# Linear attention into a soft mixture of experts: early loads joined, two batches' key-value products a tile later, one weight unit loaded by itself

## The chip, the core and the metric

The kernel runs on one core of one Trainium2 chip. The metric is device microseconds of one execution; the median of three runs stands for the kernel.

## What is computed

```python
def _attn_ref(q, k, v, g_norm):                       # q, k, v: 8 batches x 8 heads x 576 x 64
    kv = np.einsum('bhsd,bhse->bhde', k, v)
    out = np.einsum('bhsd,bhde->bhse', q, kv)
    rms = np.sqrt(np.mean(out * out, axis=-1, keepdims=True) + 1e-06)
    return (out / rms * g_norm).astype(np.float32)

def _moe_ref(x, phi, w1, w2):                         # x: 4608 x 512, 8 experts, 4 slots each, 1024 wide
    logits = x @ phi
    d = np.exp(logits - logits.max(0, keepdims=True))
    d /= d.sum(0, keepdims=True) + 1e-09
    slot_input = (d.T @ x).reshape(E, S_per_e, D)
    for e in range(E):
        h = np.maximum(slot_input[e] @ w1[e], 0.0)
        slot_out[e] = h @ w2[e]
    c = np.exp(logits - logits.max(1, keepdims=True))
    c /= c.sum(1, keepdims=True) + 1e-09
    return (c @ slot_out.reshape(n_slots, D)).astype(np.float32)
```

The attention's output, its heads side by side, is x. All is float32.

## The kernel before

x is worked on in 36 tiles of 128 tokens (`NT`). Nine tiles are two batches; tile 4 of each nine holds the ends of both. For a tile, `products` multiplies the queries with `bds[b % 2]`, a block matrix that holds a batch's key-value product and that product times phi; the result goes to one of two pairs of PSUM banks. ScalarE then squares it (`square`) and copies it out (`evict`), VectorE reduces the squares and the partial logits, GpSimd scales. Softmax over the tokens runs along in groups of six tiles (`group_max` to `group_sum`).

A batch's key-value product is made by `kv_step` in three steps: step 0 is 16 products of its first half, step 1 is 16 of its second half with 8 for the borders and a copy by ScalarE, step 2 (`slots`) transposes and fills `bds`. The table `kv_steps` (lines 625 to 628) says ahead of which tile a step stands: the key is the batch and the tile counted from the batch's first tile, `first`, which is 4 for batch 1 and 9 for batch 2. So before, step 0 of batch 1 stands ahead of tile 2 and steps 1 and 2 ahead of tile 3; the three steps of batch 2 stand ahead of tiles 6, 7 and 8. Batch 0 is done half by half ahead of tile 0 (lines 677 to 684).

After the last tile come the experts: `expert_h(e)` multiplies with w1, `expert_y(e, half)` with w2, then `gather`, `mix` and `output` write the result through four stores.

All data goes through `arena`, 160 units of 256 columns, whose parts serve one thing after the other (`KV_AT`, `Q_AT`, `W_AT`). All transfers are issued by SP, in the order in which the code stands. `load_row` loads keys, values and queries; eight such loads are issued at the start without a wait, three more behind batch 0, one behind tile 9. `load_w` loads a row of `W_ROWS`, several weight units that lie side by side, and is called behind tiles 18, 24 and 27 (`loads_behind`) and from the last part. The row that begins with half of w2's unit 2 takes units 32 to 72 of the arena, and so waits for the last reads of the last queries, which lie at 36 to 54.

The class `Order` records every operation with the cells it reads and writes, and `emit` gives each operation the waits that follow from this. A load has one semaphore; whoever reads any part of it waits for all of it. All operations are issued from one helper, so all rows of the profile say line 204.

Of the kernel before, what the change touches and what calls it, by code (L numbers as in the profile page):

```python
# [11 lines left out]
P = 128  # L12
# [15 lines left out]
TOK = 4608  # L28
# [4 lines left out]
KV_AT = (0, 36, 54, 0, 90, 126, 18, 54)  # L33
Q_AT = (18, 72, 108, 36)
# [6 lines left out]
    (("w1", 0, None), ("w1", 1, None)),  # L41
    (("w1", 2, None), ("w1", 3, None)),
    (("w1", 4, None), ("w2", 2, 1), ("w2", 0, None), ("w2", 1, None)),
    (("w2", 2, 0), ("w1", 6, None), ("w1", 5, None)),
    (("w1", 7, None),),
    (("w2", 3, None), ("w2", 4, None)),
    (("w2", 5, None), ("w2", 6, None)),
# [5 lines left out]
HEAD = 144  # L53
# [207 lines left out]
def row_length(row):  # L261
    return sum(UNIT if part is None else UNIT // 2 for _, _, part in row)


def soft_moe_linear_attention(nc, first_in, kv_in, q0_in, q1_in, kv4_in, kv5_in, t3_in, w_in, out):


    const = Const(nc)
# [9 lines left out]
    def place(at, n):  # L278
        return arena[:, HEAD + at * KB : HEAD + at * KB + n]

    def load_row(at, src):
        nc.sync.dma_start(place(at, src.shape[-1]), src)
# [14 lines left out]
    def homes(kind, u):  # L297
        at = W_AT[kind, u]
        if at is None:
            return [xflat[:, :UNIT]]  # L300
        return [place(a, UNIT // len(at)) for a in at]

    def load_w(kind, u, part=None):
        i = [row[0] for row in W_ROWS].index((kind, u, part))
        lo = sum(row_length(row) for row in W_ROWS[:i])
        n = row_length(W_ROWS[i])
        src = w_in[:, lo * P : (lo + n) * P].rearrange("o (p n) -> (o p) n", p=P)
        t = homes(kind, u)[part or 0]
        if n > t.shape[-1]:
            t = place(W_AT[kind, u][part or 0], n)  # L310
        nc.sync.dma_start(t, src)

    def w_block(kind, u, i):
# [4 lines left out]


    nc.sync.dma_start(arena[:, : HEAD + 2304], first_in)  # L320
    load_row(KV_AT[0] + 9, kv_in[0, :, 2304:])
    load_row(Q_AT[0], q0_in[:, :2048])
    load_row(KV_AT[1], kv_in[1, :, :2304])
    load_row(KV_AT[1] + 9, kv_in[1, :, 2304:])
    load_row(Q_AT[0] + 8, q0_in[:, 2048:])
    load_row(KV_AT[2], kv_in[2])
    load_row(Q_AT[1], q1_in)


    loads_behind = {  # L330
# [1 line left out]
        18: lambda: load_w("w1", 0),  # L332
        24: lambda: load_w("w1", 2),
        27: lambda: load_w("w1", 4),
    }

    nc.scalar.preload_act_table_set("natural_log_exp_and_others")
# [285 lines left out]
    first = {b: 9 * (b // 2) + 4 * (b % 2) for b in range(B)}  # L623
    kvs = {}
    kv_steps = {(b, i - 3): (i,) for b in range(2, B) for i in range(3)}
    kv_steps.update({(1, -2): (0,), (1, -1): (1, 2)})
    kv_steps.update({(6, i - 4): (i,) for i in range(3)})
    del kv_steps[6, -1]

# [20 lines left out]
    def fill(n, cols=256, home=None):  # L650

        if not n:
            return
        t = home if home is not None else ps.tile([P, 2, 512], F32, tag="o", name="fill", bufs=2)[:, 1]
        for i in range(n):
            nc.tensor.matmul(
                t[:, :cols].rearrange("p (a n) -> p a n", n=256),
                lhsT=zeros[:, :P],
                rhs=zeros.unsqueeze(1).to_broadcast([P, cols // 256, 256]),
                start=True,  # L660
                stop=True,
            )
# [14 lines left out]
    for g in range(2):  # L677
        kv = Kv(0, "o" if g else "kv", 2 if g else None)
# [3 lines left out]
        fill(1, cols=512)  # L682
        kv.slots((g,))
        fill(EARLY[1 + g], cols=512)
    load_row(KV_AT[3], kv_in[3])
    load_row(Q_AT[1] + 8, kv4_in)
    load_row(Q_AT[2], kv5_in)
    T_at, diag_at, pb_at, d_at, sums_at = {}, {}, {}, {}, {}
# [274 lines left out]
def build_program():  # L963
    import concourse.bacc as bacc

    nc = bacc.Bacc("TRN2", target_bir_lowering=False, num_devices=1, dynamic_dma_scratch_size=SCRATCH)
    shapes = {
        "first": (P, HEAD + 2304), "kv": (4, P, TOK), "q0": (P, TOK), "q1": (P, 2048),
        "kv4": (P, 2560 + TOK), "kv5": (P, 2 * TOK), "t3": (P, 3 * TOK),
        "w": (1, 2 * NE * P * UNIT),  # L970
    }
    args = [nc.dram_tensor(f"in_{n}_dram", s, F32, kind="ExternalInput").ap() for n, s in shapes.items()]
    args.append(nc.dram_tensor("out_0_dram", (1, 4 * NCH * P * 4 * CT * NS), F32, kind="ExternalOutput").ap())
    order = Order(nc)
    soft_moe_linear_attention(order, *args)
    order.emit()
    return nc
# [58 lines left out]
```

## Time and profile before

| | |
|---|---|
| median of 3 runs | 172.49 us (172.42 to 172.51) |
| the profiled execution | 172.53 us, of which span 171.2 us |
| TensorE busy | 149.1 us, 87% |
| ScalarE / VectorE / GpSimd busy | 52% / 50% / 33% |
| moved by DMA | 71.67 MB, mean 419 GB/s |
| granted TensorE clock, mean | 0.979 |

The span is the time from the first to the last instruction of the program; 1.3 us of the execution lie around it. Times in the rows below are microseconds from the span's start. PE is TensorE's matmuls, PEld its weight loads, SPq the queue of SP, which issues the transfers. One float32 matmul of the code stands as two in the counts.

### The profile page before, as it was taken

Reading aid. Unit: us, or ns where it says so; the run is one execution under the profiler, and the core shown is the slowest. Engines: PE = TensorE matmul, PEld = TensorE weight load, DVE = VectorE, ACT = ScalarE, POOL = GpSimd, SP = SyncE. Lnnn points to the kernel's source line nnn. Section 1 sums busy time; section 2 is a strip of 40 time slices with the busy share of each in tenths; the row PEclk is TensorE's granted clock in tenths of the full one; section 3 lists DMA queues with packets and bytes.
Section 4 is the critical chain, followed back from the end, with each engine's and each line's share of the span. In section 5 each row is a group of like instructions: output and inputs, shape, how many; then the busy total and the mean of one; then the engine's idle time right before and its main releaser. Section 6 shows DMA issues by size and latency. Waiting matters only on the chain.

```text
span 171.2 us, 4497 instructions
## 1 busy us (share of the span) xinstructions
PE 149.1 (87%) x1975; PEld 108.1 (63%) x1975; DVE 86.0 (50%) x184; ACT 88.9 (52%) x230; POOL 57.2 (33%) x68
## 2 busy tenths in 40 slices
PE   7787897989999899999899999999999988989400
PEld 3467776979688888898797775455565444445100
DVE  1122156283677265763936798724897027137400
ACT  2037576786965887768849864203213025137400
POOL 6000708548356755466482579200000000000000
PEclk9999999999999999999999999999999999999965
DMA  5999999999999999999999999998999999999995
GB/s 192 416 422 433 439 415 437 472 421 474 417 413 458 430 426 430 406 404 452 433 492 419 431 429 389 434 450 354 436 478 387 461 390 421 439 396 439 406 459 241
DMA packets 3476, 71.67 MB, mean 419 GB/s; under 512 B 384, under 2 KB 384, under 8 KB 384
## 3 DMA queue, kind: packets, MB, share of 16 engines
q1 hardware_dynamic: 3456, 71.38, 97.6%
q8 instruction: 15, 0.25, 0.5%
q14 instruction: 5, 0.04, 0.1%
HBM read 61.94 MB, written 9.44 MB: 417 GB/s over the span
## 4 chain that ended last, share of the span: by engine, by line
PE 47%; DMA 26%; ACT 12%; DVE 5%; SPq 2%; issue 1%
PE psum L204 47%; DMA arena<-in_kv_dram 13%; DMA arena<-in_w_dram 13%; ACT bd L204 3%; ACT sq L204 3%; ACT xall L204 2%; SPq L204 2%; DVE logits L204 1%; ACT arena L204 1%; DVE ms L204 1%; ACT part L204 1%; ACT d L204 1%; ACT r L204 1%; DVE r L204 0%; DVE d L204 0%
## 5 line engine op out<-in xcount | busy, mean ns | idle before, releaser
L204 PE MATMUL psum<-bd,arena 128*128 128x192 f32 (+1 forms) x320 | 56.1, 335 | 1.9 <-ACT bd L204 1.5
L204 PEld LDWEIGHTS psum<-bd,arena 128*128 128x128 f32 (+1 forms) x320 | 45.4, 179 | 7.1 <-ACT bd L204 2.8
L204 DVE TENSOR_REDUCE ms<-sq 128x16 f32<-128x1024 f32 (+1 forms) x19 | 22.1, 1162 | 32.6 <-ACT sq L204 32.3
L204 POOL TENSOR_TENSOR xall<-xall,r 128x512 f32<-128x512 f32 x34 | 34.8, 1044 | 0.0
L204 POOL TENSOR_TENSOR part<-part,r 128x512 f32<-128x512 f32 x17 | 17.8, 1049 | 49.7 <-DVE r L204 49.7
L204 ACT ACTIVATE sq<-psum 128x512 f32<-128x512 f32 x36 | 21.5, 598 | 12.6 <-PE psum L204 12.4
L204 PE MATMUL psum<-arena 128*64 128x64 f32 (+1 forms) x640 | 21.7, 226 | 3.3 <-DMA arena<-in_kv_dram 2.2
L204 PEld LDWEIGHTS psum<-arena 128*64 128x64 f32 (+1 forms) x640 | 19.0, 137 | 7.9 <-DMA arena<-in_kv_dram 3.5
L204 ACT COPY xall<-psum 128x512 f32<-128x512 f32 x34 | 20.6, 606 | 0.0
L204 ACT COPY part<-psum 128x256 f32<-128x256 f32 (+1 forms) x38 | 13.6, 359 | 9.9 <-DVE part L204 8.8
L204 DVE TENSOR_REDUCE logits<-part 128x64 f32<-128x512 f32 (+1 forms) x18 | 17.8, 991 | 0.0
L204 PE MATMUL psum<-arena,xall 128*32 128x256 f32 x256 | 15.0, 380 | 0.4 <-DMA arena<-in_w_dram 0.2
L204 DVE COPY arena<-psum 128x768 f32<-128x768 f32 (+1 forms) x12 | 10.4, 889 | 8.4 <-PE psum L204 8.4
L204 ACT COPY arena<-psum 128x768 f32<-128x768 f32 (+1 forms) x14 | 10.1, 755 | 8.3 <-PE psum L204 8.3
L204 PE MATMUL psum<-logits,part 32*128 32x384 f32 x96 | 12.8, 521 | 1.5 <-ACT arena L204 0.9
L204 PE MATMUL psum<-arena,sq 128*32 128x256 f32 x224 | 12.7, 379 | 0.2 <-DVE sq L204 0.2
L204 PEld LDWEIGHTS psum<-arena,xall 128*32 128x32 f32 x256 | 8.0, 110 | 7.3 <-DMA arena<-in_w_dram 1.8
L204 PE MATMUL psum<-xall,d 128*32 128x129 f32 x288 | 10.8, 278 | 0.9 <-ACT d L204 0.9
L204 ACT COPY bd<-psum 64x128 f32<-64x128 f32 (+1 forms) x32 | 9.9, 309 | 1.6 <-PE psum L204 1.4
L204 PEld LDWEIGHTS psum<-logits,part 32*128 32x128 f32 x96 | 6.1, 183 | 7.1 <-ACT arena L204 4.2
L204 PEld LDWEIGHTS psum<-arena,sq 128*32 128x32 f32 x224 | 7.2, 110 | 5.2 <-DVE sq L204 0.6
L204 PEld LDWEIGHTS psum<-xall,d 128*32 128x32 f32 x288 | 7.0, 109 | 4.1 <-ACT d L204 2.2
(74 smaller groups left out, 118.9 us busy)
## 6 DMA issues: line engine op xcount, KB each, us to landing
arena<-in_w_dram SPq DMA_DIRECT2D x4, 4096.0 KB, 19.9
arena<-in_w_dram SPq DMA_DIRECT2D x1, 7168.0 KB, 27.5
arena<-in_t_dram SPq DMA_DIRECT2D x1, 6912.0 KB, 36.1
arena<-in_w_dram SPq DMA_DIRECT2D x1, 5120.0 KB, 17.9
arena<-in_kv_dram SPq DMA_DIRECT2D x2, 2304.0 KB, 23.4
arena<-in_kv_dram SPq DMA_DIRECT2D x1, 4608.0 KB, 42.6
out_dram<-arena SPq DMA_DIRECT2D x2, 2304.0 KB, 9.6
arena<-in_kv_dram SPq DMA_DIRECT2D x1, 3584.0 KB, 32.2
```

The lines of the kernel that those rows point to most:

```text
L204: inst = getattr(engine, method)(*args, **kwargs)
```

## The change

Six of the eight first loads become three. The second half of batch 0 and the first part of q0 are one load (`kq0`, 2176 KB); the two halves of batch 1 are one (2304 KB); batch 2 and the first part of q1 are one (`kq2`, 3328 KB). They go to the same places of the arena, which lie side by side. The arrays are put together on the host so that each partition's row is one piece.

The products of batch 1 all stand ahead of tile 3, and those of batch 2 ahead of tile 7 (steps 0 and 1) and tile 8.

The weight row of half of w2's unit 2, w1's unit 6 and w1's unit 5 (5120 KB) is split: w1's unit 5 (2048 KB) is a row of its own, loaded behind tile 30, and the other two (3072 KB) stay where the whole row was loaded.

```diff
@@ W_ROWS
     (("w1", 4, None), ("w2", 2, 1), ("w2", 0, None), ("w2", 1, None)),
-    (("w2", 2, 0), ("w1", 6, None), ("w1", 5, None)),
+    (("w1", 5, None),),
+    (("w2", 2, 0), ("w1", 6, None)),
     (("w1", 7, None),),
@@ soft_moe_linear_attention
     nc.sync.dma_start(arena[:, : HEAD + 2304], first_in)
-    load_row(KV_AT[0] + 9, kv_in[0, :, 2304:])
-    load_row(Q_AT[0], q0_in[:, :2048])
-    load_row(KV_AT[1], kv_in[1, :, :2304])
-    load_row(KV_AT[1] + 9, kv_in[1, :, 2304:])
-    load_row(Q_AT[0] + 8, q0_in[:, 2048:])
-    load_row(KV_AT[2], kv_in[2])
-    load_row(Q_AT[1], q1_in)
+    load_row(KV_AT[0] + 9, kq0_in)
+    load_row(KV_AT[1], kv1_in)
+    load_row(Q_AT[0] + 8, q0_in)
+    load_row(KV_AT[2], kq2_in)
...
         27: lambda: load_w("w1", 4),
+        30: lambda: load_w("w1", 5),
     }
...
-    kv_steps.update({(1, -2): (0,), (1, -1): (1, 2)})
+    kv_steps.update({(1, -1): (0, 1, 2)})
+    kv_steps.update({(2, -2): (0, 1), (2, -1): (2,)})
+    del kv_steps[2, -3]
     kv_steps.update({(6, i - 4): (i,) for i in range(3)})
...
-    load_row(KV_AT[3], kv_in[3])
+    load_row(KV_AT[3], kv3_in)
```

TensorE from batch 0's second half to tile 7, before. A tile is four products 128x192 with `bd` (eight 64x192 for tile 4); the 64x64 products are a batch's, 16 for step 0 and 24 for step 1.

```order
L204 MATMUL psum<-bd,arena 128x192 x8
L204 MATMUL psum<-arena 64x64 x16
L204 MATMUL psum<-bd,arena 128x192 x4
L204 MATMUL psum<-arena 64x64 x24
L204 MATMUL psum<-ident,kvT 128x128 x2
L204 MATMUL psum<-gphi,kvT 128x128 x2
L204 MATMUL psum<-bd,arena 128x192 x4
L204 MATMUL psum<-bd,arena 64x192 x8
L204 MATMUL psum<-bd,arena 128x192 x4
L204 MATMUL psum<-arena 64x64 x16
L204 MATMUL psum<-bd,arena 128x192 x4
L204 MATMUL psum<-arena 64x64 x24
```

The same stretch of TensorE in the change, from tiles 0 to 2 to tile 7:

```order
L205 MATMUL psum<-bd,arena 128x192 x12
L205 MATMUL psum<-arena 64x64 x40
L205 MATMUL psum<-ident,kvT 128x128 x2
L205 MATMUL psum<-gphi,kvT 128x128 x2
L205 MATMUL psum<-bd,arena 128x192 x4
L205 MATMUL psum<-bd,arena 64x192 x8
L205 MATMUL psum<-bd,arena 128x192 x8
L205 MATMUL psum<-arena 64x64 x40
L205 MATMUL psum<-bd,arena 128x192 x4
```

Tile 2 now stands ahead of all of batch 1's products, and tile 6 ahead of all of batch 2's.

SP's first loads, before (columns are elements of each partition's row):

```order
L204 DMA arena<-in_first_dram 128x2448
L204 DMA arena<-in_kv_dram 128x2304
L204 DMA arena<-in_q_dram 128x2048
L204 DMA arena<-in_kv_dram 128x2304 x2
L204 DMA arena<-in_q_dram 128x2560
L204 DMA arena<-in_kv_dram 128x4608
L204 DMA arena<-in_q_dram 128x2048
L204 DMA arena<-in_kv_dram 128x4608
```

SP's first loads in the change:

```order
L205 DMA arena<-in_first_dram 128x2448
L205 DMA arena<-in_kq_dram 128x4352
L205 DMA arena<-in_kv_dram 128x4608
L205 DMA arena<-in_q_dram 128x2560
L205 DMA arena<-in_kq_dram 128x6656
L205 DMA arena<-in_kv_dram 128x4608
```

Of eight loads ahead of batch 3's five are left; the order of the bytes is the same.

SP's weight loads in the change, from w1's units 0 to 3 to w2's units 3 to 6, with what each waits for:

```order
L205 DMA arena<-in_w_dram 128x8192 [waits done_tensor] x2
L205 DMA arena<-in_w_dram 128x14336 [waits done_tensor]
L205 DMA arena<-in_w_dram 128x4096 [waits done_tensor]
L205 DMA arena<-in_w_dram 128x6144 [waits done_tensor]
L205 DMA xall<-in_w_dram 128x4096 [waits done_tensor]
L205 DMA arena<-in_w_dram 128x8192 [waits done_tensor] x2
```

The rows of 4096 and 6144 were one of 10240 at the place of the second.

## Rows read from the trace of the kernel before

**Rows 1.** The page's list of DMA queues: packets, MB, share of 16 engines' span.

```profile
q1 hardware_dynamic: 3456, 71.38, 97.6%
q8 instruction: 15, 0.25, 0.5%
```

**Rows 2.** Windows: length, five engines' busy us, granted clock, DMA share, GB/s.

```profile
11.50:26.70 15.20, 12.19 (x142) 10.42 (x142) 4.84 (x12) 10.13 (x28) 3.92 (x4) 1.00 1.01 426
...
104.00:106.00 2.00, 2.00 (x24) 1.08 (x17) 1.90 (x6) 0.59 (x3) 1.84 (x4) 1.00 0.80 328
...
151.00:153.00 2.00, 1.89 (x33) 0.89 (x32) 0.44 (x2) 0.48 (x1) 0.00 (x0) 1.00 0.85 359
...
161.00:162.00 1.00, 0.00 (x0) 0.00 (x0) 0.11 (x1) 0.08 (x1) 0.00 (x0) 1.00 0.87 369
...
163.00:169.00 6.00, 0.00 (x0) 0.00 (x0) 0.00 (x0) 0.00 (x0) 0.00 (x0) 0.60 0.98 422
```

**Rows 3.** The chain that ended last: the page's sum, one link (start, us).

```profile
PE 47%; DMA 26%; ACT 12%; DVE 5%; SPq 2%; issue 1%
...
122.21 22.24 DMA arena<-in_w_dram
```

**Rows 4.** The page's DMA issues: count, KB each, us from issue to landing.

```profile
out_dram<-arena SPq DMA_DIRECT2D x1, 3072.0 KB, 9.9
...
out_dram<-arena SPq DMA_DIRECT2D x1, 1536.0 KB, 6.8
```

**Rows 5.** Timeline of SP: start, us, transfers issued (x2: first of two).

```profile
0.74 0.38 SPq L204 DMA_DIRECT2D arena<-in_first_dram  x1
...
1.64 0.42 SPq L204 DMA_DIRECT2D arena<-in_q_dram  x1
...
4.30 0.72 SPq L204 DMA_DIRECT2D arena<-in_q_dram  x1
...
157.04 4.48 SPq L204 DMA_DIRECT2D out_dram<-arena  x2
...
161.19 0.33 SPq L204 DMA_DIRECT2D out_dram<-arena  x1
```

**Rows 6.** A window at the span's start, columns as in rows 2.

```profile
1.20:1.70 0.50, 0.50 (x2) 0.15 (x1) 0.36 (x1) 0.50 (x1) 0.29 (x3) 1.00 0.00 0
```

**Rows 7.** The three loads of queries q0 and q1, from issue to landing.

```profile
DMA to landing us min/median/max: 9.9/17.9/24.8
```

**Rows 8.** Timeline of TensorE, 8 to 32: start, us, count [idle before, releaser].

```profile
8.59 0.38 PE L204 MATMUL psum<-zeros 128*128 128x512 bf16 x1
9.10 1.43 PE L204 MATMUL psum<-arena 128*64 128x64 f32 x40
...
11.86 2.87 PE L204 MATMUL psum<-bd,arena 128*128 128x192 f32 x16 [0.40 <-ACT bd L204]
15.61 1.15 PE L204 MATMUL psum<-arena 128*64 128x64 f32 x32 [0.88 <-DMA arena<-in_kv_dram]
...
18.19 1.54 PE L204 MATMUL psum<-arena 128*64 128x64 f32 x48
...
20.95 4.47 PE L204 MATMUL psum<-bd,arena 128*128 128x192 f32 x32
26.70 1.15 PE L204 MATMUL psum<-arena 128*64 128x64 f32 x32 [1.28 <-DMA arena<-in_kv_dram]
...
29.28 1.54 PE L204 MATMUL psum<-arena 128*64 128x64 f32 x48
30.75 1.57 PE L204 MATMUL psum<-bd,arena 128*128 128x192 f32 x8
```

**Rows 9.** Timeline of TensorE, 134 to 149, columns as in rows 8.

```profile
134.67 3.66 PE L204 MATMUL psum<-arena,xall 128*32 128x256 f32 x64 [0.25 <-DMA arena<-in_w_dram]
...
143.40 0.97 PE L204 MATMUL psum<-logits,part 32*128 32x384 f32 x8 [0.36 <-DVE arena L204]
144.49 3.66 PE L204 MATMUL psum<-arena,xall 128*32 128x256 f32 x64
```

More of the change, by code (lines that the diff above doesn't have):

```diff
@@ L262, in row_length, with soft_moe_linear_attention @@
     return sum(UNIT if part is None else UNIT // 2 for _, _, part in row)
-def soft_moe_linear_attention(nc, first_in, kv_in, q0_in, q1_in, kv4_in, kv5_in, t3_in, w_in, out):
+def soft_moe_linear_attention(nc, first_in, kq0_in, kv1_in, q0_in, kq2_in, kv3_in, kv4_in, kv5_in, t3_in, w_in, out):
     const = Const(nc)
@@ L967, in build_program @@
     shapes = {
-        "first": (P, HEAD + 2304), "kv": (4, P, TOK), "q0": (P, TOK), "q1": (P, 2048),
+        "first": (P, HEAD + 2304), "kq0": (P, 2304 + 2048), "kv1": (P, TOK), "q0": (P, 2560),
+        "kq2": (P, TOK + 2048), "kv3": (P, TOK),
         "kv4": (P, 2560 + TOK), "kv5": (P, 2 * TOK), "t3": (P, 3 * TOK),
@@ L1017 @@
         "in_first_dram": first,
-        "in_kv_dram": kv[:4],
-        "in_q0_dram": qm[0],
-        "in_q1_dram": np.ascontiguousarray(qm[1][:, :2048]),
+        "in_kq0_dram": np.concatenate([kv[0][:, 2304:], qm[0][:, :2048]], axis=1),
+        "in_kv1_dram": kv[1],
+        "in_q0_dram": np.ascontiguousarray(qm[0][:, 2048:]),
+        "in_kq2_dram": np.concatenate([kv[2], qm[1][:, :2048]], axis=1),
+        "in_kv3_dram": kv[3],
         "in_kv4_dram": np.concatenate([qm[1][:, 2048:], kv[4]], axis=1),
```

## The prediction

> **What bounds the kernel now.** I read the queue list of the page first, then the windows, then the chain of waits, then the early and the late timeline. The queue list says that loads and stores keep the 16 DMA engines at work for 97.6% of the span [rows 1]. The windows say that this holds stage by stage: the DMA share is 1.01 in 11.50:26.70, and it falls clearly only in three places, 104.00:106.00 (0.80), 151.00:153.00 (0.85) and 161.00:162.00 (0.87) [rows 2]. (Packets are booked where they start, so a share may read a little over 1.) So this kernel is a stream of 71 MB through one queue, and an engine of the core matters only where it issues a transfer too late to keep the stream fed.
>
> The chain of waits says otherwise at first sight: nearly half of it is TensorE. But its last long link is a DMA: the w2 load that SP issues at 122.21 lands 22.24 us later [rows 3]. It stood in the queue behind other loads; issued some us later it would have landed at the same time. TensorE's work before 122.21 is therefore not what sets the end, though the chain runs through it. What follows that landing is: TensorE's products at 144.49, the outputs, the last store issued at 161.19, which lands 9.9 us later and ends the span [rows 4, 5, 9].
>
> **How late may the last store be?** The store before it, issued at 157.04, lands 6.8 us later, at 163.84; the last lands at 161.19 + 9.9 = 171.09 [rows 4, 5]. Between the two landings lie 7.25 us for 3072 KB, 2.36 us per 1000 KB, which is the pace of the stream: the DMA engine that finishes last had no pause. Others had: the share of 0.87 in 161.00:162.00. A first packet starts about 1 us after its issue (the first load is issued at 0.74, and nothing moves yet in 1.20:1.70 [rows 5, 6]), so the last store was ready by about 162.2, and the last engine took it up no later than 163.84. Its margin lies between 0 and 1.6 us. A part of the 1.6 is the time from the last packet to the landing; I take 1.2, near the upper end, because the two landings follow each other at the full pace.
>
> **The change part by part.**
>
> *Bytes.* None are added or taken away, so the stream keeps its length. This is the main term, and it is zero.
>
> *Six loads into three, one weight row into two.* 24 transfers become 22. The price of a transfer in a full queue is read from landings that follow each other. q0's first part, 1024 KB, lands at 1.64 + 9.9 = 11.54, 2.44 us after batch 0's second half was taken up at 9.10; q1's 1024 KB land at 4.30 + 24.8 = 29.10, 2.40 us after batch 2 was taken up at 26.70 [rows 5, 7, 8]. That is 2.34 to 2.38 us per 1000 KB against 2.36 for the 3072 KB store. The pairs differ from the store by 1% at most, and the 7808 KB that are joined are 18.4 us at its pace; 1% is 0.2, and I let the bound be 0.3 for the rounding of the landings. So the gain lies between 0 and 0.3; I take 0.1, near the rows that show none. The weight row's split gives a third of it back, 0.03. Net -0.07 us. SP's issues are three fewer, but off the path, since the queue is already fed when it gives out the later ones.
>
> *By a rule of the Trainium skill this term would be far larger.* DMA: Bandwidth & Descriptors, section Anatomy of one DMA, gives each transfer a fixed cost of about 2.0 us; two transfers fewer would be an estimate of 4.0 us, and 168.5 us in all. The page fits that to single transfers issued from GpSimd; the landings here, 2.4 us apart for 1.05 MB, leave no room for it.
>
> *The joined loads land later for whoever wanted their first half.* TensorE used to take up batch 0's second half at 9.10; now this lands with q0, at about 11.5, so everything on TensorE from there is 2.4 us late: tile 0 starts at 14.25, not at 11.86 [rows 8]. How much of that stays is worked out with durations of the same rows (a tile takes 1.49, 4.47 for three). Before, TensorE waited in this stretch for batch 1, with 0.88 of idle time ahead of 15.61, again for its second half at 18.19, and for batch 2, with 1.28 ahead of 26.70. Now tiles 0 to 2 follow each other from 14.25 to about 18.75. Batch 1 has landed by 18.19, so its 40 products begin at once; they take 1.15 + 1.54 less 0.14 of overlap, 2.55 us, and with the 1.2 from there to the next tile (18.19 + 1.54 to 20.95) tile 3 begins at 22.5: 1.55 late. Tiles 3 to 6 now run before batch 2 is wanted, 6 us from 22.5, with up to 0.6 for ScalarE's evictions, and end between 28.5 and 29.1. Batch 2 with q1 lands at 29.1 as well. Its 2.55 us of products end at 31.65, and tile 7 starts there and not at 30.75 [rows 8]: **0.9 us late**, no less, since the landing sets that, and up to 2.4 if nothing is caught up.
>
> *What the 0.9 us do later.* I find no wait for a load from here to 132, so they stay. Every load that SP issues behind TensorE's reads goes out 0.9 us later, and the full queue covers that. The one thin spot, at 104 [rows 2], gets w1 5 put before it: 2048 KB, by 2.36 us per 1000 KB 4.8 us of stream, issued behind tile 30 and not behind the last tile that reads the queries. SP waits there for batch 7's last reads, made a tile before, and what is queued behind it goes out later anyway. What it can gain is the idle 0.2 of 2 us, 0.4; I take 0, since the engines that stand dry are those that are ahead, and the end belongs to the last. On TensorE the 0.9 meet a wait of 0.25 for w2 at 134.67 and later 0.1 between 143.40 + 0.97 and 144.49 [rows 9]. 0.55 are left there and at the last store: issued at 161.75, inside the margin of 1.2. Cost 0; with a margin of 0 it would be 0.55.
>
> **Sum.** 172.53 us of the profiled execution (171.2 of it span) - 0.07 = 172.46. That execution is 0.04 above the median of 172.49, so the median should go to **172.4**. 0.2%, here 0.35 us, is about what a measurement of this kernel can tell from no change.
>
> **The rivals.**
>
> *Slower: the outputs overtake the stream.* Tiles 3 to 6 catch up nothing, because ScalarE's evictions or the reductions behind them hold them. Then 2.4 - 0.35 = 2.05 us reach the last store, 0.85 past the margin: 173.3. It decides from a delay of 1.55 at tile 7; with a margin of 0 from 0.35, and then the 0.9 I expect give 173.0. For it: the dips at 151 and 161 show stores issued just in time. Against it: the idle 0.88 and 1.28 of rows 8 are there to be used up. Chance 0.14.
>
> *Slower: the clock falls.* TensorE will idle from 8.97 (8.59 + 0.38) to 11.5, 2.5 us. Against it: after 161 TensorE does nothing, and the granted clock is still 1.00 in 161.00:162.00 and 0.60 on the mean of 163.00:169.00, so it fell to its half near 164.2 [rows 2], over 3 us later. If it fell to 1.2 GHz at tile 0, that tile alone would cost 1.5 more, the delay would pass 2.4, and the time be 173.3 and up. Chance 0.04. The Trainium skill speaks for this rival: TensorE: Matmul & The Clock Gate, section HAM oscillation, tells of waits for DMAs that drop the clock to half round after round; no run here shows that yet.
>
> *Faster: transfers have a price after all.* At the upper bounds, 0.3 for the joined loads and some of the 0.4 at 104: 171.8 to 172.1. Chance 0.08. With the page's 2 us for each, 168.5, chance 0.01.
>
> *Either way: instruction packets.* 15 of them take 0.5% of 16 engines' span, 13.7 us in all or 0.9 each on one engine [rows 1]. Which engine has how many decides which is last. If TensorE's shorter program shifts them, the end moves by 0.9: 171.6 or 173.4, chance 0.025 each.
>
> *The change does not do what it says:* w1 5 goes out earlier but lands where it would have, ahead of the same row. The time is then the forecast, and it is counted there.
>
> **How the numbers follow.** Forecast 0.68, its own range 172.2 to 172.7. Faster 0.08 + 0.01 + 0.025, 0.12 with rounding; slower 0.14 + 0.04 + 0.025, 0.20 with rounding. The range reaches to the faster case below and to the slower one with a thin margin above, 172.0 to 173.0; left out are slower cases past 173.0 and the odd ones, under 2 in 10.
>
> **What would show it.** In the trace after: TensorE takes up batch 0's second half at 11.5 and starts tile 0 near 14.2; the waits for batch 1 vanish; batch 2's products start near 29.1, tile 7 near 31.6; the wait at 134.67 is gone; the last store goes out 0.5 us later than 161.19 and lands within 0.2 us of before. A tile 7 past 32.5, with a DMA share well under 0.8 around the last store's issue, would prove the slower rival. A last landing before 170.7 would mean that transfers cost more than I allow, or that other engines are last.

## The result, and the profile after

The change made the kernel 0.5% slower: 173.89 us median of 19 executions against 172.57 of 19 of the kernel before. The ratio is 1.0054, 95% interval 1.0028 to 1.0080. (Ratios leave out executions over 1.5% above the fastest of their kernel; here those are the two longest, 175.04 and 175.13, and in later series of the kernel before three odd ones of 181 to 493 us.) The prediction said 172.4, range 172.0 to 173.0, so it was wrong.

The median hides two kinds of executions. The 19 before lie between 172.38 and 172.80. Those after spread from 172.36 to 175.13, and they follow TensorE's mean granted clock:

| mean granted clock | executions of after | time, us |
|---|---|---|
| 0.972 to 0.980 | 6 | 172.36 to 172.79 |
| 0.953 to 0.967 | 13 | 172.70, 172.97, and eleven from 173.86 to 175.13 |

The profiled execution is one of the first kind: 172.36 us, span 171.0, clock 0.980. Its queues, to be held against [rows 1] (packets, MB, share of 16 engines):

```profile
q1 hardware_dynamic: 3168, 71.38, 97.6%
q8 instruction: 15, 0.25, 0.5%
```

Its TensorE timeline, to be held against [rows 8] and [rows 9] (start, us, engine, line, operation, count, in brackets the idle time before and what ended it):

```profile
9.05 0.38 PE L205 MATMUL psum<-zeros 128*128 128x512 bf16 x1
11.22 1.43 PE L205 MATMUL psum<-arena 128*64 128x64 f32 x40 [1.80 <-DMA arena<-in_kq_dram]
13.98 4.58 PE L205 MATMUL psum<-bd,arena 128*128 128x192 f32 x24 [0.40 <-ACT bd L205]
...
22.18 4.47 PE L205 MATMUL psum<-bd,arena 128*128 128x192 f32 x32
...
28.97 2.48 PE L205 MATMUL psum<-arena 128*64 128x64 f32 x80
31.38 1.57 PE L205 MATMUL psum<-bd,arena 128*128 128x192 f32 x8
...
134.97 3.66 PE L205 MATMUL psum<-arena,xall 128*32 128x256 f32 x64
...
144.61 3.66 PE L205 MATMUL psum<-arena,xall 128*32 128x256 f32 x64
```

And SP's issues of the row of w1's units 2 and 3 (w1 2 and w1 3 from here on) and of the last store, the latter to be held against [rows 5]:

```profile
75.44 0.33 SPq L205 DMA_DIRECT2D arena<-in_w_dram  x1
...
161.30 0.33 SPq L205 DMA_DIRECT2D out_dram<-arena  x1
```

This execution does what was forecast. The joined load is taken up at 11.22, tile 0 starts at 13.98, tile 7 at 31.38 (before: 30.75), the wait of 0.25 ahead of 134.67 is gone, and the last store goes out 0.11 us later than before. Nothing in it is slow. The longer executions have to be looked at themselves.

A second series of the same kernel gave one whose profile is a long one: 175.15 us, span 173.8, clock 0.956. Its TensorE timeline:

```profile
8.29 0.38 PE L205 MATMUL psum<-zeros 128*128 128x512 bf16 x1
11.25 1.94 PE L205 MATMUL psum<-arena 128*64 128x64 f32 x40 [2.58 <-DMA arena<-in_kq_dram]
14.67 6.12 PE L205 MATMUL psum<-bd,arena 128*128 128x192 f32 x24 [0.19 <-ACT bd L205]
...
24.41 4.47 PE L205 MATMUL psum<-bd,arena 128*128 128x192 f32 x32
...
31.13 2.48 PE L205 MATMUL psum<-arena 128*64 128x64 f32 x80
33.54 1.57 PE L205 MATMUL psum<-bd,arena 128*128 128x192 f32 x8
```

The same stretch of it by windows (stretch, its length; then busy time of PE, PEld, DVE, ACT and POOL with counts; granted clock, DMA share, GB/s):

```profile
9.00:11.50 2.50, 0.25 (x8) 0.25 (x10) 0.00 (x0) 0.00 (x0) 0.00 (x0) 1.00 1.00 429
11.50:11.80 0.30, 0.30 (x18) 0.30 (x15) 0.00 (x0) 0.00 (x0) 0.00 (x0) 1.00 0.57 246
11.90:18.60 6.70, 6.51 (x42) 5.63 (x39) 0.44 (x2) 1.75 (x6) 0.00 (x0) 0.50 1.01 429
18.70:25.00 6.30, 5.81 (x103) 5.38 (x102) 1.74 (x4) 4.58 (x13) 2.33 (x3) 1.00 1.02 438
```

TensorE stands for 2.58 us until the joined load lands. It begins batch 0's second half, and about 0.6 us later its granted clock goes from 1.00 to 0.50, 2.4 to 1.2 GHz, and stays there through 18.60. Tiles 0 to 2 take 6.12 us and not 4.58. Tile 7 starts at 33.54, 2.16 later than in the short execution (172.36) and 2.79 later than before. The loads are not at fault: the DMA share in 11.90:18.60 is 1.01.

### The profile page after: what moved, and what is told of

Its sections match the earlier page's. It is cut to its first block, busy times and chain, and to the rows that moved or that the text cites. A ratio compares the mean times of both kernels' runs of the same rounds, so it can differ in the third digit from the quotient of the medians.

```text
span 171.0 us, 4495 instructions
## 1 busy us (share of the span) xinstructions
PE 150.2 (88%) x1975; PEld 108.4 (63%) x1975; DVE 86.0 (50%) x184; ACT 88.6 (52%) x230; POOL 57.1 (33%) x68
## 3 DMA queue, kind: packets, MB, share of 16 engines
q1 hardware_dynamic: 3168, 71.38, 97.6%
## 4 chain that ended last, share of the span: by engine, by line
PE 64%; ACT 16%; DVE 7%; DMA 6%; issue 1%; SPq 0%
PE psum L205 64%; DMA arena<-in_kq_dram 6%; ACT sq L205 4%; ACT bd L205 4%; ACT xall L205 3%; DVE ms L205 2%; ACT arena L205 2%; DVE logits L205 1%; ACT part L205 1%; ACT r L205 1%; DVE arena L205 1%; ACT d L205 1%; DVE part L205 1%; DVE r L205 0%; ACT kvT L205 0%
## 5 line engine op out<-in xcount | busy, mean ns | idle before, releaser
L205 ACT COPY kvT<-psum 128x256 f32<-128x256 f32 (+1 forms) x9 | 3.1, 349 | 12.7 <-PE psum L205 12.7
```

The source lines that it names most:

```text
L205: inst = getattr(engine, method)(*args, **kwargs)
```

## From a late tile 7 to a late end

Behind tile 7 both executions run TensorE at the full clock, and the lateness stays. It reaches two transfers. SP's issues in the long execution:

```profile
77.61 0.33 SPq L205 DMA_DIRECT2D arena<-in_w_dram  x1
...
163.75 0.33 SPq L205 DMA_DIRECT2D out_dram<-arena  x1
```

The same row's issue before:

```profile
74.82 0.33 SPq L204 DMA_DIRECT2D arena<-in_w_dram  x1
```

What the stream moves about the first of them, in the long execution (stretch, length, PE busy with count, clock, DMA share, GB/s):

```profile
79.00:80.00 1.00, 1.00 (x10) 1.00 0.67 262
80.00:81.00 1.00, 1.00 (x7) 1.00 0.92 393
```

And in the short execution:

```profile
79.00:80.00 1.00, 1.00 (x19) 1.00 1.17 492
80.00:81.00 1.00, 1.00 (x11) 1.00 1.06 459
```

The row w1 2 with w1 3 is issued behind tile 24. Issued at 77.61 it reaches a queue that runs thin: 262 GB/s in 79.00:80.00, where the short execution has 492. (One microsecond is a coarse measure, since a packet's bytes are booked where it starts; over 76.00:92.00 the figures are 407 and 430, shown further down.) A transfer's landings on the 16 DMA engines tell what this costs. "Last" is the engine that lands last; the fourth column is an experiment below, in which w1 2 has gone out earlier and the row is w1 3 alone. SP's issues of that row and of the last store in it:

```profile
77.59 0.33 SPq L206 DMA_DIRECT2D arena<-in_w_dram  x1
...
163.44 0.33 SPq L206 DMA_DIRECT2D out_dram<-arena  x1
```

| us | before | after | after, long execution | w1 2 issued earlier, clock fallen |
|---|---|---|---|---|
| the load ahead of it has landed, last | 80.10 | 79.93 | 80.00 | 84.73 |
| w1 2 and 3 issued | 74.82 | 75.44 | 77.61 | 77.59 |
| landed, last | 89.83 | 89.61 | 92.27 | 89.64 |
| third store landed, last | 163.83 | 163.66 | 166.43 | 164.54 |
| last store issued | 161.19 | 161.30 | 163.75 | 163.44 |
| last store landed, middle engine | 169.74 | 169.84 | 172.30 | 171.99 |
| last store landed, last | 171.06 | 170.89 | 173.68 | 172.06 |

In the long execution the last engine lands the row 2.4 us later than before, and it is 2.6 us late at the third store and at the last. From the third store to the last it takes 7.25 us (173.68 - 166.43), as before (171.06 - 163.83 = 7.23): it had no pause at the stores. So the lateness was made ahead of the stores, and it begins at this row. It does not all come from there, though. Two loads further on the last landing is only 1.3 us behind that of the short execution (114.02 against 112.76), and at the load after that 2.8 (122.84 against 120.03): there the last engine was set back by another 1.6. An instruction packet starts in that stretch, at 120.06, and such packets set back one engine each in the trace before, too (last section), so I put the 1.6 down to it. The row and the place of that packet then made the 2.6 together. That it is one engine all the way is inferred from the spacing; the landings bear no names.

The other engines show the second cost, the late stores. Where the row is early (fourth column) all 16 engines land the last store within 0.16 us, the last 8.62 us after its issue (172.06 - 163.44): the store alone sets the end. In the long execution 14 of 16 land it in 172.22 to 172.38, which is 163.75 + 8.62 = 172.37. So the late stores alone would have cost 172.37 - 171.06 = 1.3 us, the late row with that packet costs 2.6 on one engine, and the later of the two counts. The longest profile of all, that with three fillers below, shows the same: the row goes out at 77.88, its last engine takes 12.98 from the landing before, and at the end 15 engines land in 172.84 to 173.00, as the last store's issue at 164.38 and its 8.62 give, and one at 174.30.

## Experiments

The kernel has fillers ahead of its waits: products of zeros that nobody reads, whose only use is to keep TensorE at work. `EARLY` counts them around batch 0; its middle number stands between batch 0's halves, where the new wait is.

**The same kernel again**, nothing edited, for a second series of executions.

> The changed kernel as it stands, once more. Theory C (the clock falls): while TensorE waits for the joined load of batch 0's second half and q0 (9.4 to 11.2 in the trace), its clock drops to 1.2 GHz in some executions and stays there for some us. Then the times spread from 172.4 to about 175, the longer ones with a lower mean granted clock (0.98 down to 0.953), and a trace of a long execution shows a granted clock of 0.50 somewhere between 7 and 20, tile 7 later than 31.4 by 2 us or more, and the last store issued later than 162.5. Theory P (the place of the products): the clock is not the cause; the moved products or the split weight row make the end sensitive to small shifts; a long execution then shows a granted clock of 1.00 between 4 and 40 and loses its time later.

Measured: 174.07 median (172.45 to 175.19, 12), ratio 1.0056 (1.0024 to 1.0088), 8 of 12 above 173. The slowdown repeats, and this gave the long profile read above. The times follow the clock again: 0.977 and above 172.45 to 172.54, at 0.963 174.00, at 0.953 175.19.

**Eight fillers more in the new wait.** The load lands as late, but TensorE does not stand still.

```diff
-EARLY = (5, 1, 0)
+EARLY = (5, 9, 0)
```

> The changed kernel with 8 more filler matmuls (128x512, 0.215 us each) ahead of the wait for the joined load, so that TensorE works through it. Theory C: no drop, all executions between 172.2 and 172.8, mean granted clock 0.97 to 0.98, ratio to before 0.998 to 1.000. Theory P: spread as in the changed kernel, 172.4 to 175, median about 173.9.

Measured: 172.54 (172.23 to 172.76, 11), ratio 0.9998 (0.9989 to 1.0007), clock 0.973 to 0.982, none above 173. TensorE's timeline of this run:

```profile
8.81 2.11 PE L205 MATMUL psum<-zeros 128*128 128x512 bf16 x9
11.28 1.43 PE L205 MATMUL psum<-arena 128*64 128x64 f32 x40 [0.37 <-DMA arena<-in_kq_dram]
14.04 4.57 PE L205 MATMUL psum<-bd,arena 128*128 128x192 f32 x24 [0.40 <-ACT bd L205]
...
31.49 1.57 PE L205 MATMUL psum<-bd,arena 128*128 128x192 f32 x8
```

The delay of an execution that keeps its clock is all there (11.28, 14.04, 31.49) and costs nothing. Without the clock's fall there is no slowdown: the fall is the cause, and the delay by itself is hidden, as forecast.

**The joined load alone, put into the kernel before** (its array is put together on the host, as in the change); the other loads, the steps and the weight rows stay.

```diff
-    load_row(KV_AT[0] + 9, kv_in[0, :, 2304:])
-    load_row(Q_AT[0], q0_in[:, :2048])
+    load_row(KV_AT[0] + 9, kq0_in)
```

> The kernel before with one join alone: batch 0's second half and q0's first part as one load. Theory C: this wait alone makes the spread, so times from 172.4 to about 175 and a median above 173. Theory P: as before, 172.4 to 172.8.

Measured: 174.70 median of nine executions. Eight lie between 172.84 and 175.77, six of them above 173, and all eight have a clock of 0.953 to 0.970; the ninth took 197.64 at a clock of 0.747 and tells nothing of the join. Ratio 1.0084 (1.0046 to 1.0122). The profiled execution, TensorE's timeline:

```profile
11.21 2.40 PE L204 MATMUL psum<-arena 128*64 128x64 f32 x40 [2.56 <-DMA arena<-in_kq_dram]
...
31.68 1.57 PE L204 MATMUL psum<-bd,arena 128*128 128x192 f32 x8
```

and a window of it (columns as in the first windows above):

```profile
11.00:14.40 3.40, 3.19 (x43) 2.61 (x44) 0.00 (x0) 0.27 (x1) 0.00 (x0) 0.50 1.02 434
```

This one join is enough for the whole slowdown. In this execution the clock fell for the shorter stretch of 11.00 to 14.40, tile 7 starts 0.93 later than before, and the time is 172.98.

**The change without that join**: the same joined array, loaded by two transfers.

```diff
-    load_row(KV_AT[0] + 9, kq0_in)
+    load_row(KV_AT[0] + 9, kq0_in[:, :2304])
+    load_row(Q_AT[0], kq0_in[:, 2304:])
```

> The changed kernel with that one load taken apart again; the two other joins, the moved products and the split weight row stay. Theory C: no spread, 172.2 to 172.8, ratio to before 0.998 to 1.000. Theory P: spread as in the changed kernel.

Measured: 172.48 (172.37 to 173.03, 11), ratio 0.9995 (0.9985 to 1.0004). Undoing the join takes the slowdown away, though one execution lies above the 172.8 that was expected. The timeline has the early wait no more, but one for batch 1:

```profile
9.15 1.43 PE L205 MATMUL psum<-arena 128*64 128x64 f32 x40
...
18.05 2.48 PE L205 MATMUL psum<-arena 128*64 128x64 f32 x80 [1.57 <-DMA arena<-in_kv_dram]
```

Two of the 11 executions have a clock of 0.963 and 0.965, with 173.03 and 172.69. Whether that shorter wait is what the clock falls behind there can't be said, since neither was profiled.

**No filler, two more, and four more.** Three sizes of the same thing; the first is

```diff
-EARLY = (5, 1, 0)
+EARLY = (5, 0, 0)
```

The other two have 3 and 5 for the middle number.

> The changed kernel with the one filler ahead of the wait taken out, so that TensorE idles 0.4 us longer. Theory C: the clock falls in at least as many executions as in the changed kernel (20 of 31 above 173 so far): two thirds or more above 173, median 174 to 174.7. If the idle time had nothing to do with it: as the changed kernel, or better by the filler's time.

> The changed kernel with 2 more fillers ahead of the wait (4 more sufficed: 172.34 to 172.96). Theory C with a limit between 1 more and 4 more: some executions above 173, fewer than in the changed kernel, and each with a mean granted clock under 0.97. If any filler at all sufficed: none.

> The changed kernel with 4 more filler matmuls ahead of the wait for the joined load, half as many as in the run with 8. The filler is then over about 0.9 us after TensorE's last product and 0.9 to 1.7 us of idle time are left. Theory C (the clock falls when too much of a stretch is idle): fewer or no executions with a fallen clock; if the idle time has to exceed what is left, all between 172.2 and 172.9; at most a quarter of the executions above 173. Theory that only a filled wait helps: still a third or more above 173.

| fillers there | median (range, executions) | ratio (interval) | above 173 |
|---|---|---|---|
| 0 | 173.37 (172.48 to 175.41, 12) | 1.0042 (1.0022 to 1.0063) | 8 of 12 |
| 1 (the change, both series) | 173.89, 174.07 (172.36 to 175.19, 31) | 1.0054, 1.0056 | 19 of 31 |
| 3 | 173.89 (172.40 to 175.77, 12) | 1.0071 (1.0044 to 1.0099) | 10 of 12 |
| 5 | 172.51 (172.34 to 172.96, 11) | 1.0001 (0.9992 to 1.0010) | 0 of 11 |
| 9 | 172.54 (172.23 to 172.76, 11) | 0.9998 (0.9989 to 1.0007) | 0 of 11 |

The profiled execution without a filler is a short one (172.50); from its timeline:

```profile
8.80 0.39 PE L205 MATMUL psum<-gphi,kvT 128*128 128x128 f32 x2
11.25 1.43 PE L205 MATMUL psum<-arena 128*64 128x64 f32 x40 [2.06 <-DMA arena<-in_kq_dram]
```

With three fillers it is the longest of all, 175.77; TensorE's timeline:

```profile
8.62 0.81 PE L205 MATMUL psum<-zeros 128*128 128x512 bf16 x3
11.28 1.43 PE L205 MATMUL psum<-arena 128*64 128x64 f32 x40 [1.85 <-DMA arena<-in_kq_dram]
14.19 6.88 PE L205 MATMUL psum<-bd,arena 128*128 128x192 f32 x24 [0.19 <-ACT bd L205]
```

and its window of tiles 0 to 2, where the clock is 0.52:

```profile
14.00:20.00 6.00, 5.81 (x19) 5.81 (x20) 0.44 (x2) 1.77 (x5) 0.00 (x0) 0.52 1.03 435
```

With five, TensorE's timeline:

```profile
8.42 1.24 PE L205 MATMUL psum<-zeros 128*128 128x512 bf16 x5
11.37 1.43 PE L205 MATMUL psum<-arena 128*64 128x64 f32 x40 [1.71 <-DMA arena<-in_kq_dram]
```

With five fillers the slowdown is gone, though 1.71 us of idle time are left. Two of the three expectations missed. Without a filler two thirds are above 173 as expected, but the median is 173.37 and not 174 to 174.7; with two more, fewer long executions were expected, all at a clock under 0.97, and there are more, two of them at 0.971. (The 20 of 31 in the first text is a miscount; it is 19.) So the count of long executions doesn't fall evenly with the idle time: an idle time of 1.85 had the fall behind it here, one of 2.06 had not. What else decides is not settled by these runs. It isn't the chip: 0 and 3 fillers ran on one chip and 1 (second series), 5 and 9 on another, but five fillers also ran on the first, in the last experiment below, with none of 11 above 173.

**w1 2 issued earlier**, to test the path from the late tile 7 to the end: the row behind tile 24 is split, and its first half goes out behind tile 19.

```diff
-    (("w1", 2, None), ("w1", 3, None)),
+    (("w1", 2, None),),
+    (("w1", 3, None),),
...
-        24: lambda: load_w("w1", 2),
+        19: lambda: load_w("w1", 2),
+        24: lambda: load_w("w1", 3),
```

> The changed kernel, its clock left to fall, with the row of w1's units 2 and 3 split, so that unit 2 is loaded behind tile 19 and only unit 3 waits for tile 24. In the long execution the row's issue came at 77.61, when the first engines were through with the load before it (78.12), and the DMA share should show a gap there. Theory S (the late issue starves the stream, and that adds to the end): the long executions become shorter, from about 175 to 173.5 to 174; the short ones stay at 172.4. Theory O (only the last stores come late, the stream has nothing to do with it): no change, up to 175.2, median about 174.

Measured: 172.77 (172.35 to 174.94, 12), ratio 1.0023 (1.0000 to 1.0045). The clock still falls: in eight of 12 it is below 0.97. But of these, seven with 0.957 to 0.966 end at 172.36 to 173.97, where in the two series of the unsplit kernel 0.953 to 0.967 meant up to 175.19. At equal clocks the split shows best: at 0.957 to 0.966 ten of 12 executions of the unsplit kernel took 173.86 or more, with the split two of seven. The eighth took 174.94 at 0.923, a clock that no execution of the change had; it was not profiled. The profiled one, 2.78 us late at tile 7 against before:

```profile
33.53 1.57 PE L206 MATMUL psum<-bd,arena 128*128 128x192 f32 x8
```

Its window about the split row (columns as in the first windows above; the last number is GB/s):

```profile
76.00:92.00 16.00, 15.43 (x234) 13.33 (x233) 9.69 (x20) 11.89 (x33) 10.24 (x12) 1.00 1.04 443
```

The same window of the change's long execution and of its short one:

```profile
76.00:92.00 16.00, 15.42 (x234) 13.32 (x233) 9.68 (x20) 11.89 (x33) 10.25 (x12) 1.00 1.00 407
...
76.00:92.00 16.00, 15.42 (x198) 13.50 (x197) 9.27 (x20) 11.75 (x34) 9.15 (x9) 1.00 1.01 430
```

And of the kernel before:

```profile
76.00:92.00 16.00, 15.43 (x197) 13.23 (x195) 9.26 (x21) 11.99 (x34) 9.16 (x9) 1.00 1.02 440
```

With the split the starved row is gone (443 GB/s, not 407), and what is left is the late stores: span 172.2, 1.0 more than before. So the end has the two causes read from the table of landings. Against the long execution of the change the last landing comes 1.6 us earlier (172.06, 173.68), and 0.3 of that is the earlier last store; this is one pair of profiles.

**The other two parts alone, in the kernel before.** First the steps of batches 1 and 2 a tile later:

```diff
-    kv_steps.update({(1, -2): (0,), (1, -1): (1, 2)})
+    kv_steps.update({(1, -1): (0, 1, 2)})
+    kv_steps.update({(2, -2): (0, 1), (2, -1): (2,)})
+    del kv_steps[2, -3]
```

> The kernel before with the moved products alone (batch 1's ahead of tile 3, batch 2's ahead of tiles 7 and 8), all loads as they were. Theory C: no spread, 172.2 to 172.8, ratio 0.999 to 1.001; tile 7 within 1 us of 30.75. If the order of the products were the cause: a median above 173.

Measured: 172.63 (172.37 to 172.99, 10), ratio 1.0003 (0.9994 to 1.0012). Tile 7 starts earlier than before's 30.75, and that is worth nothing at the end; from its TensorE timeline:

```profile
30.32 1.57 PE L204 MATMUL psum<-bd,arena 128*128 128x192 f32 x8
```

Then w1's unit 5 by itself, behind tile 30:

```diff
-    (("w2", 2, 0), ("w1", 6, None), ("w1", 5, None)),
+    (("w1", 5, None),),
+    (("w2", 2, 0), ("w1", 6, None)),
...
+        30: lambda: load_w("w1", 5),
```

> The kernel before with the split weight row alone, w1's unit 5 loaded behind tile 30. Theory C: no change, 172.2 to 172.8, ratio 0.999 to 1.001; the DMA share in 104 to 106 rises from 0.80 to about 1 and the end does not move. If the dry engines at 104 mattered: up to 0.4 us faster.

Measured: 172.60 (172.40 to 172.73, 10), ratio 1.0000 (0.9991 to 1.0009). The dip at 104 does not go away; its window reads deeper than in [rows 2]:

```profile
104.00:106.00 2.00, 2.00 (x20) 1.02 (x13) 1.91 (x6) 0.48 (x3) 1.84 (x4) 1.00 0.45 193
```

**A version that might beat both**: four fillers more and w1 2 issued earlier, both edits as above.

> 4 more fillers and the row of w1's units 2 and 3 split as in the run with unit 2 behind tile 19, on top of the changed kernel: no fallen clock and no thin place at 78. If the stream alone sets the end, 172.3 to 172.9 and a ratio to before of 0.998 to 1.000; a gain of more than 0.3 us would say that dry engines at 78 and 104 cost something in the kernel before.

Measured: 172.46 (172.34 to 172.60, 11), ratio 0.9994 (0.9985 to 1.0002). It repairs the change and gains nothing that can be told from none. With the clock held up and the queue fed nothing but the stream is seen to set the end, before and after.

## Why the prediction was wrong

*Bytes: right.* 71.38 MB, 97.6% and 15 instruction packets, as before.

*The joins' price: right as far as can be seen.* Net -0.07 us was forecast. The change with eight fillers more, in which nothing else differs, came out at 0.9998, about 0.03 us less, with 0.2 to either side. One join more or less (172.54 with the join and fillers, 172.48 with two transfers) does not show. The Trainium skill's fixed 2.0 us for each transfer (DMA: Bandwidth & Descriptors, section Anatomy of one DMA) is not borne out in this full queue, as the prediction expected.

*Where the joined loads land, and what TensorE does then: right while the clock holds.* Forecast and measured in the profiled execution of after: tile 0 at 14.25 and 13.98, tile 3 at 22.5 and 22.18, batch 2's products at 29.1 and 28.97, tile 7 at 31.65 and 31.38.

*The margin of the last store: right.* It was taken as 1.2 us. A last store that nothing holds back needs 8.62 from issue to the last landing (the fourth column of the landings), so before's, which landed at 171.06, could have gone out at 162.44, 1.25 after its 161.19. The prediction's rows gave only 0 to 1.6, so that 1.2 came this close is in part luck.

*The dip at 104: right, for a reason half seen.* It was priced at 0 because the engines that stand dry are ahead. In after the same stretch reads 0.43, and 161.00:162.00 reads 0.69, in an execution that is no longer than before's (windows of after, columns as above):

```profile
104.00:106.00 2.00, 2.00 (x46) 1.38 (x37) 1.58 (x6) 0.80 (x4) 1.76 (x5) 1.00 0.43 184
...
161.00:162.00 1.00, 0.00 (x0) 0.00 (x0) 0.23 (x1) 0.19 (x1) 0.00 (x0) 1.00 0.69 295
```

Packets are booked at their start; in a stretch of 1 or 2 us such a share is no measure of an idle queue. Over 98.00:112.00 it is 0.93 before and 0.95 in after.

*The clock: wrong, and this is the step that failed.* The forecast let TensorE keep its full clock through the new wait. The rival was on the list with the right mechanism, place and sign ("if it fell to 1.2 GHz at tile 0 ... 173.3 and up"), and got 0.04. It was put aside by one row: at the span's end the clock stayed at 1.00 for over 3 us after TensorE's last work, and the new idle time was put at 2.5. That row tells of one fall, at the end of a kernel that had kept the full clock for some 160 us; when the new wait begins, TensorE has had it for only 2.2 to 4.4 us (the last section says when it rose). The profiles show the fall behind an idle time of 2.58, of 2.56, of 2.55 (w1 2 issued earlier) and, with three fillers, of 1.85 us, and 19 of 31 executions of the change were long by their times. Why so short an idle time can bring the fall here stays open; the short time at the full clock doesn't explain it by itself, since the two profiles of the wait that kept the clock had had it for less long. The Trainium skill's section on HAM oscillation (TensorE: Matmul & The Clock Gate), which the prediction named and gave little weight, says that waits for DMAs drop the clock to half; the long executions agree, 1.00 to 0.50.

*The cost of the fall: under-sized.* "1.5 at tile 0, 173.3 and up" was the price. Measured: 2.16 us at tile 7, and eleven of 19 times from 173.86 to 175.13. The part that was missed is the cover. "Every load that SP issues behind TensorE's reads goes out 0.9 us later, and the full queue covers that" holds for 0.9, and was not asked again for 2.8. In the first two columns of the landings the row w1 2 and 3 goes out 5.3 and 4.5 us before the queue ahead of it is done (80.10 - 74.82, 79.93 - 75.44) and costs nothing; at 2.4 (80.00 - 77.61) its last landing came 2.4 us later. The other part is the margin, and it was priced rightly: a last store 2.56 later (163.75 - 161.19) with a margin of 1.25 costs the 1.3 of the late stores.

*Instruction packets: no shift seen.* There are 15 before and after, and the last landing of the short execution (170.89) is 0.17 from before's; that they decide with others which engine is last is borne out (last section).

*What would show it.* Of the signs named for the forecast all but one are in the profiled execution: tile 0, the vanished waits, tile 7, the last landing. The last store goes out 0.11 later and not 0.5. A single profile could not refute the forecast, because it was of the 8 executions in 19 that stayed below 173.

## What to carry to other kernels

A join that makes TensorE wait for a load has two prices: the wait, which a full queue can hide, and a clock that may fall behind it, which outlasts the wait. Where a change opens such a wait early in a kernel, keep TensorE at work through it (here four fillers more, of 0.2 us each, were enough), and look at all executions' times beside their mean granted clock before trusting one profile. When a cover is found for a delay, write down up to what delay it holds, and ask it again for every rival that delays more.

## What the runs showed of the hardware that was not expected

Executions of the same program differ in when the clock rises at the start, and this shifts the length of the wait. The trace's first stretch at 1.00 begins at 7.04 in the short execution of after and at 5.01 in the long one, and the same first products take longer in the short one (its line first):

```profile
3.16 3.62 PE L205 MATMUL psum<-ones 128*128 128x512 f32 x4
...
3.15 2.81 PE L205 MATMUL psum<-ones 128*128 128x512 f32 x4
```

So the filler stands at 9.05 in the short one and at 8.29 in the long one, and the wait for the same landing is 1.80 in the one and 2.58 in the other. The rise may have to do with the fall: of the profiles with the join and up to three fillers, the four that lost the clock had it rise at 4.20, 5.01, 5.25 and 6.07, the two that kept it at 7.04 and 7.00. With five fillers it was kept behind rises at 4.84 and 4.99. Six profiles are too few to call this a cause.

How long the clock stays down also differs from execution to execution: through 11.90:18.60 in the long execution of after, only through 11.00:14.40 in the kernel before with the one join.

A load of 4096 KB issued 2.4 us before the queue ahead of it was done did not reach all 16 DMA engines in time: the middle engine took 11.00 us from the landing before to this one, the last 12.27, where both executions in which it was issued earlier have 9.7 to 10.2.

An instruction packet sets back one DMA engine, as far as the timing tells. In the trace before, such a packet of 16 KB starts at 13.55 and takes 0.93 us; the load of batch 1's first half, on its way then, lands on 15 engines by 14.31 and on the last at 15.56. After the next packet, at 24.10, two engines are late (26.63 and 26.66, the others by 25.53). All 16 engines move a load, so the last landing depends on which engines the 15 packets have fallen on.
